# Start of an mLSTM + two-MoE kernel: clearing spread over three engines, first P ahead of the scans, unread matmuls in front

## The chip, the cores and the metric

One core of a Trainium2 chip runs the whole program. The metric is the device time of one execution in microseconds; the median of three runs of the kernel before is 531.15 us. The core has five engines that work side by side, each through its own instructions in order: TensorE (PE; its weight loads are shown as PEld), VectorE (DVE), ScalarE (ACT), GpSimd (POOL) and SyncE (SP), which here only issues transfers. They wait for each other through semaphores. On-chip memory is SBUF, and PSUM for the results of matmuls.

## The reference

Three parts, each feeding the next. The change touches only the beginning of the first, an mLSTM over 2 x 8 heads, 768 positions and a head size of 40:

```
m_new  = max(f_t + m, i_t)
C      = exp(f_t + m - m_new) * C + exp(i_t - m_new) * outer(v_t, k_t)
n      = exp(f_t + m - m_new) * n + exp(i_t - m_new) * k_t
y_t    = sigmoid(o_t) * (C q_t) / max(|n . q_t|, 1)
```

The result (1536 tokens of 320 features) goes through a mixture of 8 experts, two for each token, and then through a dense layer pair with `g = h * cos(h)`.

## The kernel before, in words

The mLSTM runs in chunks of 128 positions: six chunks for each of two batch entries, twelve steps in all, `att_step(0)` to `att_step(11)`. Inside a chunk the recurrence becomes matmuls: scores of q and k for the eight heads (`mm_s`, L247), a weight of gates for each pair of positions (`mk_w`: exponentials on ScalarE in L209, then a mask by a select on GpSimd in L210), their product P (`mk_p`, L256, on VectorE), and P times v plus the part from the state (`mm_out`, L306 and L310). `mm_state`, `mk_decay` and `mk_state` carry the state on; `mk_y` makes the output of a chunk and stores it; `rt_a` and `rt_b` do the first matmuls of the router on it.

The gates come first. `gates_a` (L82) is a row of VectorE instructions on 16 partitions: a scan for m (L90), two additions (L92, L93), a maximum (L94), and one scan per chunk for the running sum G (L96). For chunks 0 and 1, ScalarE then copies the sums (L99) into a tile that `gates_t` transposes on TensorE (L121); from chunk 2 on the sums go to DRAM instead, by a store to `gd` (L102), and come back spread over all partitions by a load of `gb` for each chunk (`load_gb`, L175). `gates_b` (L108 to L110) prepares two more rows, `gates_c` copies the transposes out (L125, L127, L128). For chunks 0 and 1, `mm_g` spreads the sums by transposes on TensorE (L196).

The order of the work is written out by hand: whatever is called first stands first in the queue of its engine. Every load and store of this stage is issued by SyncE in that order, and an issue that must wait holds up all behind it. Before step 0 the order is:

```
801  Y.dma_start(ident, cst[:, 0:128])
802  load_qk(0)   ...   load_qk(2)
808  gates_a(0, 1)  gates_b(0, 1)  gates_t(0, 1)  gates_c(0, 1)
812  mm_g(0)  mk_w(0)  mm_s(0, (0, 1))
815  gates_a(1, 2)  gates_b(1, 2)  gates_t(1, 2)
818  mm_s(0, (2, 3))
819  gates_a(2, 4)
820  gates_c(1, 2)  mk_e(0)
822  late_consts()  load_gb(2)
824  mk_p(0)
825  mm_g(1)  mk_w(1)  mm_s(1)  mk_e(1)
829  tanh_o(0)  gates_b(2, 4)
```

(Calls of several lines are drawn together here.) Step 0 then begins with the loads of chunk 3 (`loads(0)`: qk and gb of chunk 3, kv of chunk 2, the output gates of chunks 2 and 3), and each step loads ahead in the same way. The second `gates_a(4, NC)` runs at the end of step 1. Step n holds, in TensorE's order, `mm_state(n)`, the scores of chunk n + 2 interleaved with `mm_out(n)`, and the router's matmuls of chunk n - 1.

Three kinds of tiles are cleared at the start, because the loads and products fill them only in part: three qk tiles of 2048 columns (L134 to L137), two kb tiles of 512 (L141) and two st tiles of 328 (L145). GpSimd clears all of them but half of the second qk tile, which VectorE clears (L136). Each qk load waits for the clearing of its tile. `ones`, a two-byte tile for the router, is cleared at the end of step 0 (L886).

Of the kernel before, what the change touches and what calls it, by code (L numbers as in the profile page):

```python
# [9 lines left out]
FT = mybir.dt.float32  # L10
FR = mybir.dt.float32r
BF = mybir.dt.bfloat16
I32 = mybir.dt.int32
U32 = mybir.dt.uint32
AF = mybir.ActivationFunctionType
# [4 lines left out]
NH = H // 2  # L20
C = 128
# [19 lines left out]
def tile_mlstm_moe_moe2(ctx, tc, qk, kv, og, gi, gf, wcat, noise, wm1, wm2, cst, out):  # L41
    nc = tc.nc
    V, A, G, T, Y = nc.vector, nc.scalar, nc.gpsimd, nc.tensor, nc.sync

    cp = ctx.enter_context(tc.tile_pool(name="cp", bufs=1))
# [11 lines left out]
    def psS():  # L57
        return ps.tile([128, 512], FT, name="pS", tag="S", bufs=3)

    def psM():  # L60
        return ps.tile([128, 512], FT, name="pM", tag="M", bufs=1)
# [7 lines left out]
    ident = cp.tile([128, 128], FT, name="ident")  # L69
    cc_ = cp.tile([128, 341], FT, name="cc")  # L70
    A.preload_act_table_set("exp_and_others")

    g_r = cp.tile([16, C], FT, name="g_r")
    V.memset(g_r, 1.0)
# [9 lines left out]
    def gates_a(c0, c1):  # L84
        a, z = c0 * C, c1 * C
        s = slice(a, z)
        a1 = max(a, 1)
        if a == 0:
            V.memset(g_g[:, 0:1], 0.0)
        V.tensor_tensor_scan(out=g_m[:, s], data0=g_f[:, s], data1=g_i[:, s],  # L90
                             initial=(-1e30 if a == 0 else g_m[:, a - 1:a]), op0=OP.add, op1=OP.max)
        V.tensor_tensor(out=g_g[:, a1:z], in0=g_f[:, a1:z], in1=g_m[:, a1 - 1:z - 1], op=OP.add)  # L92
        V.tensor_tensor(out=g_g[:, a1:z], in0=g_g[:, a1:z], in1=g_m[:, a1:z], op=OP.subtract)  # L93
        V.tensor_scalar(g_g[:, a1:z], g_g[:, a1:z], -110.0, None, op0=OP.max)  # L94
        for c in range(c0, c1):
            V.tensor_tensor_scan(out=g_G[:, c * C:(c + 1) * C], data0=g_r, data1=g_g[:, c * C:(c + 1) * C],  # L96
                                 initial=0.0, op0=OP.mult, op1=OP.add)
        if c0 < 2:
            A.activation(gG[:, s], g_G[:, s], AF.Copy)  # L99
        if c0 >= 2:  # L100
            d0 = 0 if c0 == 2 else c0
            Y.dma_start(GD[d0:c1].rearrange("c p t -> p c t"),  # L102
                        g_G[:, d0 * C:c1 * C].rearrange("p (c t) -> p c t", t=C))
# [19 lines left out]
    def gates_c(c0, c1):  # L123
        pv = PT[c0]
        V.tensor_copy(tok[:, c0:c1, :], pv[:, :, 0:16])  # L125
        if c0 < 2:
            V.tensor_copy(tokG[:, c0:c1, :], pv[:, :, 64:80])  # L127
        A.activation(kdec[:, c0:c1, :], pv[:, :, 32:48], AF.Exp)  # L128


    NB = 3
    QKS, KBS, STS = [], [], []
    for i in range(NB):
        t = ap_.tile([128, 4, NH, C], FT, name=f"qk{i}")  # L134
        if i == 1:
            V.memset(t[:, 0:2], 0.0)  # L136
        G.memset(t[:, 2 * (i == 1):], 0.0)  # L137
        QKS.append(t)
    for i in range(2):
        t = ap_.tile([128, H, 64], FT, name=f"kb{i}")  # L140
        G.memset(t, 0.0)  # L141
        KBS.append(t)
    for i in range(2):
        t = ap_.tile([128, NH, 82], FT, name=f"st{i}")
        G.memset(t, 0.0)  # L145
        STS.append(t)
    XD = dr.tile([B * S, KW], FT, name="xd")
    KO = H * D
# [12 lines left out]
    def load_qk(n):  # L161
        if n >= 2 * NC:
            return
        b, c = divmod(n, NC)
        d = L[n]
        t = d["qk"] = QKS[n % NB]
        Y.dma_start(t[0:D, 0:3], qk[b, c, 0])
        Y.dma_start(t[64:64 + D, 1:4], qk[b, c, 1])
# [9 lines left out]
    def load_kv(n):  # L178
        if n >= 2 * NC:
            return  # L180
        b, c = divmod(n, NC)
        d = L[n]
        t = ap_.tile([128, KO + H * (D + 1)], FT, name="kv", bufs=NB)
        Y.dma_start(t, kv[b, c])
        d["k"] = t[:, 0:KO].rearrange("p (h d) -> p h d", d=D)
        d["v"] = t[:, KO:].rearrange("p (h d) -> p h d", d=D + 1)
# [26 lines left out]
    def mk_e(n):  # L213
        if n >= 2 * NC:
            return
        b, c = divmod(n, NC)
        d = L[n]
        if c:
            e = d["ge"] = ap_.tile([128, NH, C], FT, name="get", bufs=2)
            for s in range(2):  # L220
                r = slice(64 * s, 64 * s + 64)
                if n >= 2:
                    A.activation(e[r], d["gb"][r, s:H:2, :], AF.Exp)
                else:
                    for u in range(2):
                        A.activation(e[r, 2 * u:2 * u + 2, :], d["pg"][u][r, s:4:2, :], AF.Exp)
        if c < NC - 1:
            kb = d["kb"] = KBS[n % 2]
            G.tensor_tensor(out=kb[:, :, 0:D], in0=d["k"],
                            in1=kdec[:, c, b * H:b * H + H][:, :, None].to_broadcast([128, H, D]), op=OP.mult)  # L230
# [8 lines left out]
    def mm_s(n, ws=range(NH)):  # L239
        if n >= 2 * NC:  # L240
            return
        d = L[n]
        for i in ws:
            u, w = divmod(i, 2)
            if w == 0:
                d["ps", u] = psA()
            T.matmul(d["ps", u][:, 256 * w:256 * w + 256], d["qk"][:, 1, i, :],  # L247
                     d["qk"][:, 0:4:3, i, :], start=True, stop=True)

    def mk_p(n):  # L250
        if n >= 2 * NC:
            return
        d = L[n]
        d["p"] = ap_.tile([128, H, C], FT, name="ppt", bufs=2)
        for u in range(2):
            V.tensor_tensor(out=d["p"][:, 4 * u:4 * u + 4, :],  # L256
                            in0=d["ps", u].rearrange("p (h t) -> p h t", t=C),
                            in1=d["w"][:, 4 * u:4 * u + 4, :], op=OP.mult)
# [99 lines left out]


    tri = cp.tile([128, 128], BF, name="tri")  # L360
    ones = cp.tile([128, 128], BF, name="ones")
    io128 = cc_[:, 128:256]
    io32 = cc_[:, 256:288]
    tid = cc_[:, 288:300]
# [4 lines left out]
    def late_consts():  # L369
        Y.dma_start(cc_, cst[:, 128:469])  # L370
        Y.dma_start(wc, wcat)
        Y.dma_start(nz, noise)
# [426 lines left out]


    Y.dma_start(ident, cst[:, 0:128])
    load_qk(0)
    load_kv(0)
    load_qk(1)
# [11 lines left out]
    gates_b(1, 2)  # L816
    gates_t(1, 2)
    mm_s(0, (2, 3))
    gates_a(2, 4)
    gates_c(1, 2)  # L820
    mk_e(0)
    late_consts()
    load_gb(2)
    mk_p(0)
    mm_g(1)
    mk_w(1)
    mm_s(1)
# [4 lines left out]
    def loads(n):  # L832
        load_qk(n + 3)
        if n > 2 or n == 0:
            load_gb(n + 3)
        load_kv(n + 2)
        if n < 5:
            load_o(n + 1)
        if n == 2:
            load_gb(4)  # L840
            load_gb(5)

    def att_step(n):
        if n == 0:
            loads(0)
        if n:
            mk_e(n + 1)
        for f, a in pre.pop(n, []):
            f(*a)
        mm_state(n)  # L850
        if n:
            mm_s(n + 2, (0,))
        mm_out(n, (lambda w: mm_s(n + 2, (w + 1,))) if n else None)
        if n == 0:
            gates_t(2, 4)
        if n:
            rt_a(n - 1)
        mm_s(n + 2, (3,) if n else range(NH))
        for f, a in mid.pop(n, []):
            f(*a)  # L860
        if n:
            rt_b(n - 1)
        if n == 2:
            gates_t(4, NC)
        mk_state(n)
        mk_p(n + 1)
        mk_q(n + 1)
        mk_decay(n + 1)
        if n == 0:
            gates_c(2, 4)  # L870
        if n == 2:
            gates_c(4, NC)
        if n == 1:
            gates_a(4, NC)
        loads(n + 1)
        if n == 2 * NC - 1:
            mk_y(n)
        for f, a in fill.pop(n, []):
            f(*a)
        if n < 2 * NC - 1:  # L880
            mk_y(n)
        mk_w(n + 2)
        if n == 0:
            V.tensor_copy(tri, cc_[:, 0:128])
            V.tensor_copy(rb[:, 0], row0)
            V.memset(ones, 1.0)  # L886
            V.memset(os_[:, NC], 0.0)
        if n == 1:
            gates_b(4, NC)
        if n == 8:  # L890

            for p, r0, st, m in ((64, ROW0[2] + CAP2, 512, 6), (16, CAP1, 256, 2), (16, ROW1[0] + CAP1, 256, 2)):
                Y.dma_start(bass.AP(tensor=YD.tensor, offset=YD.offset + r0 * DM, ap=[[DM, p], [st * DM, m], [1, DM]]),
                            cc_[:p, None, 0:DM].to_broadcast([p, m, DM]))
# [84 lines left out]
    for f in range(12):  # L979
        k = 18 + (15 * f) // 4  # L980
# [19 lines left out]
    for k in range(K0, KM + N2 + 2):  # L1000
# [6 lines left out]
        while at.get(k):  # L1007
            f, a = at[k].pop(0)
# [8 lines left out]
    with tc.If(over > 0):  # L1017
# [9 lines left out]
        for b in range(B):  # L1027
            with tc.For_i(0, NC, 1) as it:
# [4 lines left out]
                p = psM()  # L1033
# [6 lines left out]
                for e in range(E):  # L1040
                    acc = psA()
                    for f in range(8):
                        w = mp.tile([128, FW], FT, name="wr", tag="wh", bufs=4)
                        Y.dma_start(w, wm1[e, :, f, :])
                        p = psS()
                        for k in range(3):
                            n = 64 if k == 2 else 128
                            T.matmul(p[:, :C], w[:n, 128 * k:128 * k + 128], xT[:n, 128 * k:128 * k + 128],
                                     start=(k == 0), stop=(k == 2))
# [10 lines left out]
                for f in range(16):  # L1060
                    wh, wl = W2[f // 4][:, 0, f % 4, :], W2[f // 4][:, 1, f % 4, :]
                    p = psS()
# [6 lines left out]
                t = mp.tile([128, DM], FT, name="yt", tag="yt", bufs=3)  # L1069
# [76 lines left out]
```

## Time and profile before

| | |
|---|---|
| three runs | 530.97, 531.15, 532.72 us |
| median | 531.15 us |
| profiled execution | 531.55 us |
| its span, first to last instruction | 529.9 us |
| granted TensorE clock, mean | 0.988 of full |
| TensorE busy | 494.5 us, 93% of the span |
| VectorE, ScalarE, GpSimd busy | 372.7, 325.7 and 282.2 us |

The profile is one execution, and it stands 0.4 us above the median; 1.65 us of it lie around the span. Times in its rows are counted from the first instruction. Matmuls are pipelined, so a busy TensorE need not be at its best rate. The attention stage fills about the first hundred microseconds; the experts and the dense pair, where TensorE is almost always busy, follow.

### The profile page before, as it was taken

The page shows a single profiled execution, that of the slowest core. Times are in us where ns is not written, and L with a number is a line of the kernel's source. Part 1 is how long each engine was busy: PE and PEld are TensorE (multiplying, and loading weights), DVE is VectorE, ACT ScalarE, POOL GpSimd, SP SyncE. Part 2 cuts the span into 40 slices and gives each one's busy share as a digit, 9 for nine tenths or more (in the row PEclk, how much of TensorE's full clock was granted, in tenths as well). Part 3 has the DMA queues.
Part 4 walks back from the last instruction along what each step waited for, and adds up shares of the span by engine and source line. Part 5 has one row for each costly group of instructions (what it writes and reads, how often), then busy time and mean ns, then how long its engine had stood idle before and what let it go on. Part 6 is the DMA issues. An engine that isn't in the chain of part 4 may idle for free.

```text
span 529.9 us, 9037 instructions
## 1 busy us (share of the span) xinstructions
PE 494.5 (93%) x3198; PEld 471.0 (89%) x3198; DVE 372.7 (70%) x789; ACT 325.7 (61%) x695; POOL 282.2 (53%) x248
## 2 busy tenths in 40 slices
PE   4898988898999999999999988999999999999994
PEld 2787876798999999999999987899899999999994
DVE  8874379567467776878776679678956755787772
ACT  3667565464646454545455556478777777777772
POOL 6445457668755968585868597264356347300000
PEclk9999898999999999999999998999999999999999
DMA  6889894467183928391938194030021003001001
GB/s 192 249 265 277 286 285 147 140 220 272 61 301 130 343 84 280 127 357 58 340 139 271 74 344 152 15 115 26 0 63 51 1 1 100 12 2 37 2 1 44
DMA packets 25909, 77.69 MB, mean 147 GB/s; under 512 B 3872, under 2 KB 11552, under 8 KB 25856
## 3 DMA queue, kind: packets, MB, share of 16 engines
q1 hardware_dynamic: 22752, 67.50, 36.9%
q0 software_dynamic: 3104, 9.54, 5.9%
q8 instruction: 27, 0.44, 0.3%
q14 instruction: 26, 0.21, 0.1%
HBM read 67.41 MB, written 9.62 MB: 145 GB/s over the span
## 4 chain that ended last, share of the span: by engine, by line
PE 73%; DVE 12%; ACT 5%; DMA 4%; issue 3%; POOL 1%; SPq 0%; POOLq 0%; DVEq 0%; ACTq 0%
PE pS L582 33%; PE pA L591 10%; PE pA L588 9%; PE pA L587 9%; PE pS L310 2%; PE pM L544 2%; PE pA L247 2%; DMA qk<-qk 2%; PE pA L600 1%; PE pA L599 1%; ACT wt L209 1%; PE pM L351 1%; DVE xt L667 1%; PE pS L306 1%; DMA wraw<-wm 1%
## 5 line engine op out<-in xcount | busy, mean ns | idle before, releaser
L575 POOL TENSOR_TENSOR wl<-wraw,wh 128x704 fp32r<-128x704 f32 x71 | 125.9, 1781 | 61.7 <-ACT wh L573 58.9
L637 DVE SCALAR_TENSOR_TENSOR hb<-pS,hb 128x384 fp32r<-128x384 f32 (+2 forms) x128 | 45.9, 390 | 46.3 <-ACT hb L634 43.8
L573 ACT ACTIVATE wh<-wraw 128x704 fp32r<-128x704 f32 x80 | 62.9, 786 | 15.9 <-PE pA L599 7.5
L582 PE MATMUL pS<-xh,wh 128*128 128x448 f32 (+1 forms) x240 | 69.8, 345 | 0.7 <-ACT xh L546 0.5
L582 PE MATMUL pS<-xh,wl 128*128 128x448 f32 (+1 forms) x240 | 66.6, 332 | 0.9 <-POOL wl L575 0.9
L582 PE MATMUL pS<-xh,w 128*128 128x384 f32 x288 | 66.5, 339 | 0.6 <-DVE m_t L747 0.6
L587 PE MATMUL pA<-wh,hb 128*128 128x320 f32 x208 | 62.7, 311 | 0.0
L588 PE MATMUL pA<-wl,hb 128*128 128x320 f32 x208 | 62.6, 310 | 0.0
L732 ACT ACTIVATE m_t<-pS,magic 128x384 f32<-128x384 f32 x64 | 37.1, 580 | 30.3 <-PE pS L582 25.5
L634 ACT ACTIVATE hb<-pS 128x448 fp32r<-128x448 f32 (+1 forms) x80 | 37.7, 471 | 28.8 <-PE pS L582 22.0
L582 PEld LDWEIGHTS pS<-xh,w 128*128 128x128 f32 x288 | 50.0, 188 | 1.2 <-DVE m_t L747 1.1
L591 PE MATMUL pA<-wh,hb 128*128 128x320 f32 x208 | 44.6, 314 | 3.0 <-DVE hb L637 3.0
L747 DVE SCALAR_TENSOR_TENSOR m_t<-m_t,pS 128x384 f32<-128x384 f32 x64 | 35.4, 553 | 15.4 <-ACT m_t L746 13.5
L582 PEld LDWEIGHTS pS<-xh,wl 128*128 128x128 f32 x240 | 43.2, 191 | 3.3 <-POOL wl L575 1.1
L733 DVE TENSOR_SCALAR m_t<-m_t 128x384 f32<-128x384 f32 x64 | 23.4, 365 | 28.8 <-ACT m_t L732 27.8
L582 PEld LDWEIGHTS pS<-xh,wh 128*128 128x128 f32 x240 | 40.9, 190 | 1.9 <-ACT xh L546 0.6
L753 POOL TENSOR_TENSOR wl<-m_t,wh 128x384 fp32r<-128x384 f32 x25 | 25.5, 1019 | 30.9 <-ACT wh L751 21.4
L582 PE MATMUL pS<-xl,wh 128*128 128x448 f32 (+1 forms) x160 | 39.7, 329 | 0.0
L588 PEld LDWEIGHTS pA<-wl,hb 128*128 128x128 f32 x208 | 39.0, 188 | 0.5
L587 PEld LDWEIGHTS pA<-wh,hb 128*128 128x128 f32 x208 | 38.9, 187 | 0.7
L591 PEld LDWEIGHTS pA<-wh,hb 128*128 128x128 f32 x208 | 33.3, 187 | 4.9 <-DVE hb L637 4.9
L734 DVE SCALAR_TENSOR_TENSOR m_t<-pS,m_t 128x384 f32<-128x384 f32 x64 | 35.7, 558 | 2.2
(197 smaller groups left out, 1253.7 us busy)
## 6 DMA issues: line engine op xcount, KB each, us to landing
wraw<-wm SPq DMA_DIRECT2D x36, 704.0 KB
raw<-wm SPq DMA_DIRECT2D x16, 704.0 KB
qk<-qk SPq DMA_DIRECT2D x24, 240.0 KB
gb<-gd SPq DMA_DIRECT2D x10, 512.0 KB
kv<-kv SPq DMA_DIRECT2D x12, 324.0 KB
yd<-yt SPq DMA_DIRECT2D x22, 160.0 KB
wraw<-wm SPq DMA_DIRECT2D x8, 352.0 KB
xd<-xt SPq DMA_DIRECT2D x12, 192.0 KB
```

The lines of the kernel that those rows point to most:

```text
L573: A.activation(wh, raw[:, f, :], AF.Copy)
L575: eng.tensor_tensor(out=wl, in0=raw[:, f, :], in1=wh.bitcast(FT), op=OP.subtract)
L582: T.matmul(p[:, :n], w[:, 128 * k:128 * k + 128], x[:, m, :], start=(i == 0), stop=(i == 7))
L587: T.matmul(a[:n, :DM], hh[:, s], wh[:, KW:], start=first, stop=False)
L588: T.matmul(a[:n, :DM], hh[:, s], wl[:, KW:], start=False, stop=False)
L591: T.matmul(a[:n, :DM], hl[:, s], wh[:, KW:], start=False, stop=last)
L634: A.activation(hh[:, :n], p[:, :n], AF.Relu)
L637: V.scalar_tensor_tensor(out=hb[:, o:o + z - a], in0=p[:, a:z], scalar=0.0, in1=hh[:, a:z].bitcast(FT), op0=OP.max, op1=OP.subtract)
L732: A.activation(t, m["p"], AF.Identity, bias=magic, scale=0.5 / PI)
L734: V.scalar_tensor_tensor(out=t, in0=m["p"], scalar=0.5 / PI, in1=t, op0=OP.mult, op1=OP.subtract)
L747: V.scalar_tensor_tensor(out=s, in0=s, scalar=1.0, in1=m["p"], op0=OP.subtract, op1=OP.mult)
L753: eng.tensor_tensor(out=m["hl"], in0=m["t"], in1=m["hh"].bitcast(FT), op=OP.subtract)
```

## The change

At the start, `ones` is cleared first on VectorE. The clearing is dealt out anew: GpSimd clears the first qk tile and half of the second; ScalarE clears the other half of the second and all of the third, by three copies of a zero column spread over 1024 columns; VectorE clears the zero column, kb and st. Before the first loads are issued, fourteen matmuls of `ones` with itself (384 columns each) go to TensorE, into a PSUM tile that nobody reads. And `mk_p(0)` moves from behind `late_consts` and `load_gb(2)` to just behind `mk_e(0)`, while `gates_a(2, 4)` moves from ahead of `gates_c(1, 2)` to behind `mk_p(0)`.

```diff
+    ones = cp.tile([128, 128], BF, name="ones")
+    V.memset(ones, 1.0)
...
+    zero = cp.tile([128, 1], FT, name="zero")
+    V.memset(zero, 0.0)
     for i in range(NB):
         t = ap_.tile([128, 4, NH, C], FT, name=f"qk{i}")
-        if i == 1:
-            V.memset(t[:, 0:2], 0.0)
-        G.memset(t[:, 2 * (i == 1):], 0.0)
+        if i == 0:
+            G.memset(t, 0.0)
+        else:
+            if i == 1:
+                G.memset(t[:, 0:2], 0.0)
+            for k in range(2 * (i == 1), 4, 2):
+                v = t[:, k:k + 2].rearrange("p a w t -> p (a w t)")
+                A.activation(v, zero.to_broadcast([128, 2 * NH * C]), AF.Copy)
         QKS.append(t)
     for i in range(2):
         t = ap_.tile([128, H, 64], FT, name=f"kb{i}")
-        G.memset(t, 0.0)
+        V.memset(t, 0.0)
...
         t = ap_.tile([128, NH, 82], FT, name=f"st{i}")
-        G.memset(t, 0.0)
+        V.memset(t, 0.0)
...
     Y.dma_start(ident, cst[:, 0:128])
+
+    junk = psM()
+    for i in range(14):
+        T.matmul(junk[:, 0:384], ones, ones[:, None, :].to_broadcast([128, 3, 128]), start=True, stop=True)
     load_qk(0)
...
     mm_s(0, (2, 3))
-    gates_a(2, 4)
     gates_c(1, 2)
     mk_e(0)
+    mk_p(0)
+    gates_a(2, 4)
     late_consts()
     load_gb(2)
-    mk_p(0)
     mm_g(1)
...
-            V.memset(ones, 1.0)
```

## Rows read from the trace of the kernel before

**Rows 1.** The chain that ended last, by engine (the page's part 4).

```profile
PE 73%; DVE 12%; ACT 5%; DMA 4%; issue 3%; POOL 1%; SPq 0%; POOLq 0%; DVEq 0%; ACTq 0%
```

**Rows 2.** Busy time by stretch; the last three columns: granted clock, DMA share, GB/s.

```profile
17.00:26.00 9.00, 7.86 (x60) 7.26 (x59) 7.05 (x20) 5.79 (x18) 5.18 (x9) 1.00 0.99 310
29.00:31.00 2.00, 2.00 (x20) 1.95 (x19) 0.88 (x4) 1.31 (x6) 0.00 (x0) 1.00 0.40 105
31.00:43.00 12.00, 11.37 (x86) 10.12 (x86) 8.05 (x18) 8.82 (x24) 6.87 (x12) 1.00 0.98 293
...
53.00:57.00 4.00, 4.00 (x19) 3.68 (x19) 1.14 (x2) 0.38 (x1) 1.18 (x2) 0.57 0.95 276
```

**Rows 3.** Timeline, TensorE: start, duration, instruction, idle before it and its releaser.

```profile
23.62 0.67 PE L247 MATMUL pA<-qk 128*128 128x256 f32 x2 [0.86 <-DVE st L293]
...
51.81 0.67 PE L247 MATMUL pA<-qk 128*128 128x256 f32 x2 [1.81 <-DMA qk<-qk]
...
66.27 0.30 PEld L247 LDWEIGHTS pA<-qk 128*128 128x128 f32 x2 [0.27 <-issue]
```

**Rows 4.** Timeline, SyncE's issues of transfers.

```profile
14.14 0.33 SPq L102 DMA_DIRECT2D gd<-g_all  x1
...
16.16 0.33 SPq L175 DMA_DIRECT2D gb<-gd  x1
...
28.85 0.34 SPq L102 DMA_DIRECT2D gd<-g_all  x1
```

**Rows 5.** Timeline, the clearing on VectorE and GpSimd.

```profile
0.82 4.45 POOL L137 MEMSET qk<- 128x2048 f32 x3 [0.29 <-POOLq L1139]
...
2.16 0.91 DVE L136 MEMSET qk<- 128x1024 f32 x1 [0.16 <-issue]
```

**Rows 6.** Timeline, the gates and the first P on VectorE.

```profile
3.34 0.41 DVE L90 TENSOR_TENSOR_SCAN g_all<-g_all 16x128 f32<-16x128 f32 x1 [0.26 <-DMA g_all<-gi]
...
4.41 1.38 DVE L94 TENSOR_SCALAR g_all<-g_all 16x127 f32<-16x127 f32 x1
...
8.86 0.21 DVE L94 TENSOR_SCALAR g_all<-g_all 16x128 f32<-16x128 f32 x1
...
10.36 1.05 DVE L90 TENSOR_TENSOR_SCAN g_all<-g_all 16x256 f32<-16x256 f32 x1
...
13.38 0.73 DVE L96 TENSOR_TENSOR_SCAN g_all<-g_r,g_all 16x128 f32<-16x128 f32 x2
...
14.19 1.27 DVE L256 TENSOR_TENSOR ppt<-pA,wt 128x512 f32<-128x512 f32 x2
...
15.38 0.40 DVE L108 TENSOR_TENSOR g_all<-g_all 16x256 f32<-16x256 f32 x1
...
25.38 0.73 DVE L90 TENSOR_TENSOR_SCAN g_all<-g_all 16x256 f32<-16x256 f32 x1
```

**Rows 7.** Timeline, TensorE: transposes, the two-byte matmuls of L497, long ones of L582.

```profile
7.87 1.97 PE L196 MATMUL pS<-ident,tokG 128*128 128x128 f32 x8 [0.35 <-DVE tokG L127]
...
11.58 0.40 PE L121 MATMUL pM<-ident,g_all 80*128 80x80 f32 x1
...
14.31 1.09 PE L196 MATMUL pS<-ident,tokG 128*128 128x128 f32 x8 [1.26 <-DVE tokG L127]
...
91.65 0.51 PE L497 MATMUL pM<-r_bm,r_am 128*128 128x64 bf16 x12 [0.27 <-ACT Lt L355]
...
142.91 0.36 PE L582 MATMUL pS<-xh,wh 128*128 128x448 f32 x1
143.11 0.36 PE L582 MATMUL pS<-xh,wl 128*128 128x448 f32 x1
```

**Rows 8.** Timeline, ScalarE: exponentials of chunks 0 and 2, and a 640-column activation.

```profile
9.02 2.18 ACT L209 ACTIVATE wt<-pS,tok 128x128 f32<-128x128 f32 x8 [0.92 <-PE pS L196]
...
18.36 0.74 ACT L157 ACTIVATE ogt<-ogt 128x640 f32<-128x640 f32 x1
...
20.69 2.44 ACT L209 ACTIVATE wt<-gb,tok 128x128 f32<-128x128 f32 x8
```

More of the change, by code (lines that the diff above doesn't have):

```diff
@@ L360, in tile_mlstm_moe_moe2 @@
     tri = cp.tile([128, 128], BF, name="tri")
-    ones = cp.tile([128, 128], BF, name="ones")
     io128 = cc_[:, 128:256]
```

## The prediction

> **What bounds the kernel now.** I read the chain of waits first, then the share of the DMA engines by stretch, then the waits in the timeline that the first two point to. The chain says that the whole run belongs to TensorE, 73% of it [rows 1]. That share is an average: the change touches only the first 25 us, so what counts there is which wait ends last, and what a shift there does to the rest.
>
> In the attention stage the transfers run without a pause. The sixteen DMA engines are 0.99 busy from 17 to 26 us and 0.98 from 31 to 43 [rows 2]. The one hole is 29 to 31 us, at 0.40. TensorE meets this stream three times: it waits 0.86 us at 23.62 before it may start the scores of chunk 3, 1.81 us at 51.81 and 0.27 us at 66.27 [rows 3]. The row at 51.81 names the qk load. The one at 23.62 names a VectorE instruction of L293, but `mk_state(1)` stands behind `mm_s(3, (0,))` in the code and can't hold it; what that matmul needs is its qk load, so I read this as the load too. The row at 66.27 names nothing; it is again the first score matmul of a step.
>
> What starts the stream is one instruction. SyncE issues in order, and the store of the gate sums to `gd` (L102) waits for the scans of chunks 2 and 3 on VectorE. It goes out at 14.14; the first `gb` load, which reads `gd` back, at 16.16 [rows 4]; behind it stand the loads of chunk 3 and all later ones. The next `gd` store, at 28.85, closes the hole at 29 to 31. So the time at which VectorE ends `gates_a(2, 4)` sets when the stream starts, and I follow the change to that point.
>
> **VectorE up to the first scan.** Removed is the clearing of half of qk1, 1024 columns in 0.91 us, 0.89 ns per column [rows 5]. Added are kb (2 x 512) and st (2 x 328), 1680 columns, 1.50 us at that price; `ones`, 128 columns, between 0.11 by the same price and 0.17 where it stood before, and `zero`, some 0.06. That is about 0.75 us more. The first scan (3.34 us) had waited 0.26 for the load of gi [rows 6], which is now covered, so it starts 0.5 later, at 3.85.
>
> **The stalled maximum.** The 127-column maximum of L94 took 1.38 us at 4.41, the same instruction for chunk 1 only 0.21 at 8.86 [rows 6]. It stood beside GpSimd's clearing, which went on without a break from 0.82 past 5 us [rows 5]. Now GpSimd clears 3072 columns instead of 6800, of which 5120 took the 4.45 us of their row, and is done at about 3.5, before L94 runs. I take the whole 1.17 as saved; the other end is nothing, if the stall had another cause. Net, the gates of chunk 0 are ready 0.65 earlier.
>
> **The unread matmuls.** The eight transposes of chunk 0, among the first work of TensorE, take 1.97 us, those of chunk 1 only 1.09 [rows 7]. The profile gives the granted clock as full here, but the ratio is that of its two levels, 1.2 and 2.4 GHz. Fourteen matmuls of 384 columns ahead of them should bring the full level, as the matmuls between the two rows did. Their own price isn't shown. Long matmuls of L582, 448 columns, start 0.20 apart at the full level; that is 0.17 for 384 columns and 0.34 at half the clock. The two-byte matmuls of L497, 64 columns in 0.51/12 us, give 0.26, and at half the clock 0.51 [rows 7]. I take 0.34, as the row nearest in length: 4.8 us from 1.1, over at 5.9, ahead of the gates at 6.5. At 0.51 they end at 8.2 and put off everything behind by 1.6; that end goes into the range. Were they full from the start, they would end at 3.5, which changes nothing unless the pause behind them brings the low level back. The gain at full clock is half of the 0.88 before the first exponentials of chunk 0, which start at 7.9 instead of 9.02: 1.1 earlier.
>
> **ScalarE's clearing** costs the path nothing: three copies of 1024 columns at 0.74 us per 640 columns [rows 8] are at most 3.5 us, from 2.4 to 5.9. Their cover is that ScalarE has next to nothing to do before the gates of chunk 0 are ready at 6.5. If they run over, the copy of L99 and, in SyncE's queue, the qk load of chunk 2 are late by a few tenths, and chunk 2's scores are not wanted before 18. For the clearing of `ones`, gone from the end of step 0, nothing is booked either: VectorE was not awaited there once the load of chunk 3 is.
>
> **P in front of the scans.** ScalarE needs 2.18 us for the exponentials of chunk 0 [rows 8] and only then copies the gate sums of chunk 1 (L99), which the transposes wait for. Those stood at 11.58 [rows 7] and come at 10.5. VectorE ends `gates_b(1, 2)` at about 9.7, used to go on with the scans of chunks 2 and 3 at 10.36, and now stands idle until the two copies of `gates_c(1, 2)` at 10.9. Then comes `mk_p(0)`, 1.27 us, from 11.0 to 12.3. Only then the scans start, 2.0 later than before; `mk_p` itself issues no transfer, but the scans take the `gd` store with them, and behind it on SyncE the three loads of constants, `gb` of chunk 2 and everything of step 0.
>
> The scan block took 3.75 us (10.36 to 14.11). Undisturbed, its five kinds cost 0.73 (L90 at 25.38), 0.40 twice (by L108's shape), 0.25 (L94, between rows) and 0.73 (L96), with the gaps 2.65 [rows 6]; so the three GpSimd instructions beside it cost 1.1, as the scan of L90 shows (1.05, against 0.73 undisturbed). In the new place two of GpSimd's selects for chunk 1 fall on it, 0.37 each: 3.4. The block ends at 15.7; the bounds are 14.95 undisturbed and 16.05 at the old price.
>
> The Trainium skill (SBUF — State Buffer, "Who interferes with whom") says that a VectorE instruction with two SBUF inputs and a GpSimd instruction that reads SBUF take turns, and that the one issued later waits for the whole other one. By that rule, an estimate, the block would be 2.65 if VectorE is first each time. The slow and the quick L90 agree with the rule; who comes first in the new place no row can tell.
>
> So `gd` goes out at about 15.7 instead of 14.14, **1.5 later**. What is earlier buys nothing there: the transposes of chunk 1, free of the scans, move from 14.31 to 11.6 and their exponentials with them, but step 1 waits for chunk 3's load.
>
> **What is late next.** The first `gb` load moves to 17.7, the exponentials of chunk 2 that read it from 20.69 [rows 8] to at most 22.2, TensorE's start at 23.62 to 25.1. Between the end of these exponentials (23.13) and the next scans (25.38) lie a select, products and some slack, which I put at 0.5 (an estimate). So the second `gd` store moves by 1.0, and with it the stream from 31 us on, which has no hole left that would take it up: 51.81 and 66.27 move by 1.0. TensorE, idle from about 20.5 to 25.1, will run at the low level for a while: after the 1.81 us pause its granted clock was 0.57 from 53 to 57 [rows 2], which lost 1.7 us. Its step 1 then ends some 3 us late; but it has 1.8 to give at 51.81, and where it no longer waits there, the fall at 53 to 57 goes too. So at 66.27 it waits for the loads again, and the shift is the stream's.
>
> **The sum**: the profiled execution took 531.55 us (span 529.9, 1.65 around it); with 1.0 more 532.55. It stands 0.4 above the median of 531.15, so the forecast is 532.1.
>
> **Rivals.**
> *The loads keep up (faster).* If the stream makes good the late start, TensorE goes by its own work. For it: transposes and exponentials of chunk 1 come 2.7 earlier, and the stream takes no more than 1 us of TensorE's time in the first 40. Against it: 0.99 busy. Place: TensorE at 23.62; it decides where chunk 3's load is there before 22.8. The gain lies between the 0.86 waited there and 2.7; 1.8 gives 529.4.
> *A further fall of the clock (slower).* If TensorE reaches 66.27 with nearly 2 us to wait, it falls to the low level once more, as it did behind the pause of 1.81 us. That adds 1.7 to the shift: 533.8. Against it: step 7 has slack in VectorE's router work.
> *Nothing happens.* The hole at 29 to 31 is 1.2 us of transfer time. If it takes up all of the shift, or the L94 gain is larger than I think, both ends meet: 531.2.
>
> **How the numbers follow.** Forecast 0.4, loads keep up 0.2, further fall 0.2, nothing 0.2. The range goes from 529.3, the fast rival, to 534.6, the second fall with long unread matmuls; a bit under 2 in 10 is left out. Within 0.3% is 1.6 us either way, about what can be told from no change. Faster by more: most of the fast rival and a little of low bounds, 0.2. Slower by more: nearly all of the further fall and a quarter of the forecast's own spread, 0.3. Same: 0.5.
>
> **What would show it.** In the changed kernel: L94 near 0.2 us at about 5; the first transposes in 1.1 us; `mk_p(0)` ahead of L90 at 12.3; L102 at 15.0 to 16.1; the score matmul of chunk 3 at about 25; no low clock at 53 to 57. The forecast is wrong if L102 comes before 14.5, or if it is late and the matmul at 23.6 is not.

## The result and the profile after

The change made the kernel slower: a median of 537.04 us against 531.53 us of the kernel before, six executions each, ratio 1.0101 with a 95% interval of 1.0066 to 1.0136. That lies above the forecast's range. The same program, measured once more beside the experiments, gave 1.0079 (1.0034 to 1.0123).

| | before | after |
|---|---|---|
| profiled execution | 531.55 us | 535.83 us |
| its span | 529.9 us | 534.1 us |
| granted TensorE clock, mean | 0.988 | 0.976 |
| TensorE busy | 494.5 us | 498.8 us |

The program adds only fourteen short matmuls to TensorE, which are busy for 3.7 us, and yet its span grew by 4.2 us. The chain of waits of the kernel after, by engine, gives DMA 7% where it had 4% [rows 1]:

```profile
PE 72%; DVE 11%; DMA 7%; ACT 3%; issue 3%; POOL 1%; SPq 1%; DVEq 0%; POOLq 0%; ACTq 0%
```

The timeline of the kernel after, from the start to the first `gb` load (its lines answer to [rows 4, 6, 7, 8]; line numbers have moved by 2 to 9):

```profile
1.14 3.73 PE L813 MATMUL pM<-ones 128*128 128x384 bf16 x14 [1.14 <-DVE ones L73]
...
3.86 0.41 DVE L92 TENSOR_TENSOR_SCAN g_all<-g_all 16x128 f32<-16x128 f32 x1
...
4.93 0.21 DVE L96 TENSOR_SCALAR g_all<-g_all 16x127 f32<-16x127 f32 x1
...
6.67 0.26 PE L123 MATMUL pM<-ident,g_all 80*128 80x80 f32 x1 [1.80 <-DVE g_all L112]
...
7.28 1.97 PE L205 MATMUL pS<-ident,tokG 128*128 128x128 f32 x8 [0.35 <-DVE tokG L129]
...
8.43 2.17 ACT L218 ACTIVATE wt<-pS,tok 128x128 f32<-128x128 f32 x8 [0.93 <-PE pS L205]
...
11.48 1.50 DVE L265 TENSOR_TENSOR ppt<-pA,wt 128x512 f32<-128x512 f32 x2
...
12.89 0.73 DVE L92 TENSOR_TENSOR_SCAN g_all<-g_all 16x256 f32<-16x256 f32 x1
...
13.87 0.70 POOL L219 TENSOR_SCALAR_AFFINE_SELECT wt<-wt 128x512 f32<-128x512 f32 x1 [1.87 <-ACT wt L218]
...
14.89 0.76 POOL L219 TENSOR_SCALAR_AFFINE_SELECT wt<-wt 128x512 f32<-128x512 f32 x1 [0.32 <-ACT wt L218]
15.19 1.53 DVE L98 TENSOR_TENSOR_SCAN g_all<-g_r,g_all 16x128 f32<-16x128 f32 x2
15.62 0.82 POOL L238 TENSOR_TENSOR kb<-kv,kdec 128x320 f32<-128x320 f32 x1
...
16.75 0.34 SPq L104 DMA_DIRECT2D gd<-g_all  x1
...
18.59 0.38 SPq L184 DMA_DIRECT2D gb<-gd  x1
```

Up to 6.67 it is better than before: the stalled maximum is gone (0.21 against 1.38), and the gates of chunk 0 reach TensorE about 0.5 us earlier. Then the first P (11.48) stands ahead of the scans (12.89), three GpSimd instructions fall on the scans, and the `gd` store goes out at 16.75, 2.61 later than before.

The timeline further on: TensorE's score matmuls of chunks 3 and 9 and the state matmuls of steps 2 and 8, SyncE's issues of the second `gd` and of the qk load of chunk 6, and ahead of the latter VectorE's product `qtt` of chunk 3 (`mk_q`), the last reader of the tile that it fills:

```profile
26.19 1.19 PE L256 MATMUL pA<-qk 128*128 128x256 f32 x2 [4.29 <-DMA qk<-qk]
...
30.31 0.34 SPq L104 DMA_DIRECT2D gd<-g_all  x1
...
34.41 0.88 PE L275 MATMUL pS<-kv,kb 128*104 128x82 f32 x8
...
39.92 0.75 DVE L246 TENSOR_TENSOR qtt<-qk,get 128x512 f32<-128x512 f32 x1
40.74 0.31 SPq L176 DMA_DIRECT2D qk<-qk  x1
...
69.89 1.19 PE L256 MATMUL pA<-qk 128*128 128x256 f32 x2 [2.49 <-DVE pM L403]
...
79.07 0.94 PE L275 MATMUL pS<-kv,kb 128*104 128x82 f32 x8
```

In the kernel before, the first score matmul and the second `gd` stand in [rows 3, 4]; the others are:

```profile
29.47 0.88 PE L266 MATMUL pS<-kv,kb 128*104 128x82 f32 x8
...
34.97 0.75 DVE L237 TENSOR_TENSOR qtt<-qk,get 128x512 f32<-128x512 f32 x1
35.80 0.31 SPq L167 DMA_DIRECT2D qk<-qk  x1
...
66.30 0.67 PE L247 MATMUL pA<-qk 128*128 128x256 f32 x2
...
73.91 0.94 PE L266 MATMUL pS<-kv,kb 128*104 128x82 f32 x8
```

And busy time by stretch of the kernel after (TensorE's busy time and instructions stand after the length; the last three columns are granted clock, DMA share and GB/s):

```profile
7.30:9.00 1.70, 1.70 (x8) 1.70 (x9) 1.56 (x6) 0.75 (x4) 0.00 (x0) 0.50 1.11 356
...
22.00:26.00 4.00, 0.00 (x0) 0.00 (x0) 2.35 (x9) 3.20 (x10) 1.50 (x3) 0.78 0.95 283
26.00:32.00 6.00, 5.81 (x25) 5.36 (x26) 4.15 (x8) 0.39 (x1) 0.80 (x1) 0.58 0.84 304
50.00:60.00 10.00, 9.59 (x71) 8.53 (x71) 4.87 (x11) 7.20 (x20) 4.86 (x8) 1.00 0.89 268
68.00:76.00 8.00, 6.12 (x25) 5.61 (x26) 5.93 (x33) 3.44 (x10) 3.36 (x5) 0.57 0.93 291
```

TensorE now waits 4.29 us for chunk 3's load where it had waited 0.86 [rows 3], and behind that wait two score matmuls take 1.19 us and not 0.67: it runs at the lower of its two levels (0.58 granted from 26 to 32). The wait of 1.81 at 51.81 and the low clock behind it [rows 2, 3] are gone, 50 to 60 us is at full clock. But at 69.89 comes a second long wait, 2.49 us, and a second fall. That row names a VectorE instruction of the router (L403), which a score matmul does not read; what it reads is the qk tile, so I take it for the qk load of chunk 9, which the same row names in a run below (66.38).

So the way of the lateness along TensorE is: +2.57 at the scores of chunk 3 (26.19 against 23.62); +4.94 at the state matmuls of step 2 (34.41 against 29.47), as the way between them takes 8.22 us and not 5.85; only +1.25 at step 7 (66.52 against 65.27), since the old wait and fall are gone; +3.59 at the scores of chunk 9 (69.89 against 66.30); +5.16 at step 8 (79.07 against 73.91), as the way there takes 9.18 us and not 7.61. What comes behind gives back about 1 us of it, which I didn't follow up; 4.2 is left at the end.

### The profile page after: what moved, and what is told of

It is laid out like the page before. It is cut to its first block, busy times and chain, and to the rows that moved or that the text cites. A ratio compares the mean times of both kernels' runs of the same rounds, so it can differ in the third digit from the quotient of the medians.

```text
span 534.1 us, 9067 instructions
## 1 busy us (share of the span) xinstructions
PE 498.8 (93%) x3212; PEld 473.8 (89%) x3212; DVE 372.1 (70%) x793; ACT 328.4 (61%) x698; POOL 279.1 (52%) x243
## 4 chain that ended last, share of the span: by engine, by line
PE 72%; DVE 11%; DMA 7%; ACT 3%; issue 3%; POOL 1%; SPq 1%; DVEq 0%; POOLq 0%; ACTq 0%
PE pS L590 32%; PE pA L599 10%; PE pA L595 9%; PE pA L596 9%; DMA gb<-gd 3%; PE pM L552 2%; PE pS L319 2%; PE pA L256 2%; DMA wraw<-wm 1%; PE pA L608 1%; PE pA L607 1%; DMA xgt<-xd,idx 1%; DMA qk<-qk 1%; PE pM L360 1%; ACT wt L218 1%
## 5 line engine op out<-in xcount | busy, mean ns | idle before, releaser
L256 PE MATMUL pA<-qk 128*128 128x256 f32 x96 | 32.9, 443 | 8.7 <-DMA qk<-qk 4.3
```

## The experiments

Each run was timed against the kernel before on the same chip. That kernel's executions there went from 527.8 to 539.7 us, a wider spread than in the first measurement, so tenths of a per cent can't be told apart by one run. The interval of a single run doesn't cover all of it either: the clearing alone, measured on two chips, gave two that don't meet (below).

**Which part costs?** Four kernels, each with a part of the change. First the change with P left where it was:

```diff
-    mk_p(0)
-    gates_a(2, 4)
     late_consts()
     load_gb(2)
+    mk_p(0)
...
     mm_s(0, (2, 3))
+    gates_a(2, 4)
     gates_c(1, 2)
```

> The changed kernel with the old order of mk_p(0) and gates_a(2, 4): the clearing and the unread matmuls alone. Queue theory (P ahead of the scans puts off the gd store, and with it all loads behind it; TensorE's longer waits then drop its clock): the gd store goes out at 13.4 to 13.8 us instead of 16.75, the first matmul of chunk 3's scores at about 23, and the time is that of the kernel before or a little under, 530.5 to 531.5 us. Rival (the clearing on VectorE and ScalarE or the unread matmuls cost the time): the time stays at 535 us or more though the gd store is early.

Measured: 532.84 us, ratio 0.9977 (0.9946 to 1.0008), `gd` at 13.64. The loss is gone with the move. The scores of chunk 3 start at 24.77, not at about 23, because the first `gb` load goes out only at 17.47 (the section on the prediction comes back to this). The reverse, only the move of P and the scans on the kernel before:

```diff
-    gates_a(2, 4)
     gates_c(1, 2)
     mk_e(0)
+    mk_p(0)
+    gates_a(2, 4)
     late_consts()
     load_gb(2)
-    mk_p(0)
```

> The kernel before with mk_p(0) ahead of gates_a(2, 4), nothing else. Queue theory: scans of chunks 2 and 3 start at about 13.6 us, the gd store goes out at 17.2 to 17.6 (0.5 to 0.9 later than in the changed kernel, since the stall of L94 is still there), and the time is 536 to 539 us, as slow as the whole change or slower. Rival: below 533.5 us.

Measured: 537.41 us, 1.0046 (1.0009 to 1.0083): slower, with `gd` 3.6 later than before and the same long wait ahead of the scores of chunk 3 (its row names VectorE's product P, which a score matmul does not read either). Its timeline, SyncE's `gd` and TensorE's score matmuls:

```profile
17.74 0.33 SPq L102 DMA_DIRECT2D gd<-g_all  x1
...
27.91 1.19 PE L247 MATMUL pA<-qk 128*128 128x256 f32 x2 [4.99 <-DVE ppt L256]
...
72.87 0.67 PE L247 MATMUL pA<-qk 128*128 128x256 f32 x2 [2.62 <-DMA qk<-qk]
```

The two other parts alone, the clearing and the unread matmuls (each as in the change's diff):

```diff
-        G.memset(t[:, 2 * (i == 1):], 0.0)
+                A.activation(v, zero.to_broadcast([128, 2 * NH * C]), AF.Copy)
...
-        G.memset(t, 0.0)
+        V.memset(t, 0.0)
```

> The kernel before with the new division of the clearing, nothing else. Queue theory: L94 of chunk 0 takes 0.2 instead of 1.4 us, the gd store goes out about 0.6 earlier, near 13.5, and the time is 530.5 to 531.5 us. Rival (clearing on VectorE or ScalarE costs): 533 us or more, with qk loads or the first scan late.

```diff
+    junk = psM()
+    for i in range(14):
+        T.matmul(junk[:, 0:384], ones, ones[:, None, :].to_broadcast([128, 3, 128]), start=True, stop=True)
```

> The kernel before with the clearing of ones and the fourteen unread matmuls at the start, nothing else. Queue theory: they end at 4.9 us, TensorE then stands still for over 2 us and the first transposes run at the low clock as before (about 1.97 us for eight); gd store within 0.3 us of 14.14; time within 1 us of the kernel before. Rival (the unread matmuls move the falls of the clock): a fall less or more than before, and 1.5 us or more in either direction.

Measured: the clearing alone 530.45 us, 0.99 (0.9863 to 0.9937), `gd` at 13.34, 0.80 earlier than before; the unread matmuls alone 531.17 us, 0.9964 (0.9929 to 1.0), `gd` at 14.16 as before. Neither costs anything. The move of P is the part that does; whether it makes the whole loss by itself (1.0046 against 1.0101 and 1.0079) the spread doesn't tell.

**By which way does a late `gd` cost?** In the kernel after, the qk load of chunk 3 was issued by SyncE ahead of the scans, so that it no longer stands behind the `gd` store; then the same in the kernel before:

```diff
+    load_qk(3)
     gates_a(2, 4)
...
     def loads(n):
-        load_qk(n + 3)
+        if n:
+            load_qk(n + 3)
```

> The kernel after, with the qk load of chunk 3 issued by SyncE ahead of the scans of chunks 2 and 3 and not behind the gd store. Theory (the late gd store holds the qk load of chunk 3, TensorE waits 4.3 us for it and then runs at the low clock): gd stays late, at 16.5 to 17.5, but the two qk issues come at 11 to 14; the first score matmul of chunk 3 comes at 22 to 23.5 instead of 26.19, with no wait for a qk load above 1 us there, the granted clock between 24 and 31 us rises well above the 0.5 to 0.57 of the kernel after, and 2 to 4 us of the time come back: 533 to 535 against 537. Rival (what is lost lies in the scans and P themselves, or in the unread matmuls and the clearing): the matmul comes early, but TensorE then waits as long for another link (gb, the second P), and the time stays at 536 to 538.

> The kernel before with the same early qk load. It shows what the early load is worth where gd is not late, so that it can be taken off the run beside it. Theory: the wait of 0.86 us at 23.62 goes and the scores of chunk 3 start at 22.5 to 23; gd stays at 14.1 to 14.5, the gb loads land within 0.5 us of before; the time is 0 to 1.5 us less than before (ratio 0.997 to 1.000). Rival (the row at 23.62 was not the load but VectorE): the start stays at 23.6, ratio 1.000.

Measured: in the kernel after 533.76 us, 1.0011 (0.9981 to 1.0041). The loss is gone although `gd` is nearly as late as it was. The timeline, the early load, `gd` and the scores of chunk 3, which now follow the state matmuls without a wait:

```profile
11.74 0.28 SPq L176 DMA_DIRECT2D qk<-qk  x1
...
16.28 0.33 SPq L104 DMA_DIRECT2D gd<-g_all  x1
...
22.97 0.64 PE L256 MATMUL pA<-qk 128*128 128x256 f32 x2
```

One wait and one fall of the clock are left further on (3.11 us at 44.79, 0.57 granted from 46 to 50), and yet the state matmuls of step 8 start at 74.27, only 0.36 later than before. So what the late `gd` does, it does through the load behind it. In the kernel before the same edit gained nothing: 534.72 us, 1.0023 (0.9996 to 1.0050), against my expectation. Its timeline:

```profile
14.14 0.34 SPq L102 DMA_DIRECT2D gd<-g_all  x1
...
19.06 0.80 SPq L175 DMA_DIRECT2D gb<-gd  x2
...
67.43 1.19 PE L247 MATMUL pA<-qk 128*128 128x256 f32 x2 [2.20 <-DVE xt L327]
```

The wait at 23.62 did go, but the first `gb` load, which needs the `gd` store to have landed, goes out at 19.06 and not at 16.16 [rows 4], as I read it because the early load now stands ahead of the store in the transfers; the second `gd` is 1.6 late (30.45), and a wait with a fall of the clock comes at 67.43 in place of that at 51.81. The early load moved the lateness and did not remove it. The clearing alone with the early load:

> The kernel before with the new clearing alone (no unread matmuls, P where it was) and the early qk load of chunk 3. Theory: gd at 13.3 to 13.7, scores of chunk 3 at 21.8 to 22.6 without a wait for a load, and the time below that of the clearing alone: ratio to before 0.985 to 0.993, faster than both kernels. Rival (transfers later in the stream decide, not chunk 3's load): no more than the clearing alone gave, 0.99 to 0.997.

Measured: 532.71 us, 0.9993 (0.9962 to 1.0023), `gb` at 18.93: the rival was right, the early load adds nothing to the clearing.

**How much of it is the clock?** The kernel after, with unread matmuls of 128 columns where TensorE waits, in steps 1 and 7. The loads are as late as they were:

```diff
+    FILL = {1: 72, 7: 40}
...
         mm_state(n)
+        if n in FILL:
+            L[n]["po"] = psS()
+            for i in range(FILL[n]):
+                T.matmul(L[n]["po"][:, 384:512], ones, ones, start=True, stop=True, skip_group_check=True)
```

> The kernel after, with further unread matmuls between mm_state and the score matmuls of steps 1 and 7 (72 and 40 of 128 columns), where TensorE waits 4.3 and 2.5 us for qk loads. The loads are as late as they were; what changes is what TensorE does meanwhile. Theory (two falls of the clock behind the waits are a part of the loss): the scores of chunk 3 still come at 26 to 26.5, but the granted clock behind them is 0.9 or more instead of 0.5 to 0.57, steps 2 to 4 are 2.4 to 3.2 us later than before instead of 4.95, the fall at 68 to 76 is gone, and the time is 533 to 535. Rival (the late loads alone set the time, the clock has slack): the clock is full but the shift from 74 us on stays above 4.5 us and the time at 536 to 537.5.

Measured: 533.73 us, 1.0013 (0.9987 to 1.0039). The loss is gone although the scores of chunk 3 come later still, at 27.54 and not at 26 to 26.5, `gd` goes out at 16.86, and step 2 is 3.93 later than before, more than the 2.4 to 3.2 expected. Its timeline, scores of chunk 3 and the state of step 2:

```profile
27.54 0.67 PE L256 MATMUL pA<-qk 128*128 128x256 f32 x2 [1.50 <-DMA qk<-qk]
...
33.40 0.88 PE L275 MATMUL pS<-kv,kb 128*104 128x82 f32 x8
```

Between these two rows lie 5.86 us, as in the kernel before (5.85) and not 8.22: without the fall of the clock, step 1 costs what it did. That gives the price of a fall: 2.37 us in step 1 of the kernel after, and 3.82 in its second measurement (26.74 to 36.41). For the second, the way from the scores of chunk 9 to the state of step 8 is 6.49 here (68.54 to 75.03) and 9.18 in the kernel after, 2.69 more.

Each fill alone tells how the two hang together:

```diff
-    FILL = {1: 72, 7: 40}
+    FILL = {1: 72}
```

> The kernel after with the unread matmuls of step 1 alone (72), behind which the clock fell first. If the first fall is the costly one, step 2 is 3.9 us later than before and not 4.95 to 6.9, and most of the 3.5 us that both fills gave come back: 533 to 534.5. If the second fall is the costly one, steps 2 to 4 gain 1 us or more, but from 66 us on the shift is again above 4 us and the time 535.5 to 537.5.

```diff
-    FILL = {1: 72, 7: 40}
+    FILL = {7: 40}
```

> The kernel after with the unread matmuls of step 7 alone (40). If the second fall is the costly one, steps 2 to 4 stay 5 to 7 us late, steps 6 and 7 at 1 to 3.3, and from 74 us on the shift stays below 3 us, with the granted clock there at 0.95 or more: 533 to 535. If the first fall is the costly one, 535.5 to 537.5.

Measured: step 1 alone 533.54 us, 1.0000 (0.9965 to 1.0036); step 7 alone 533.55 us, 1.0011 (0.9981 to 1.0041). Either is enough. The timelines, first of the fill in step 1:

```profile
26.36 0.67 PE L256 MATMUL pA<-qk 128*128 128x256 f32 x2 [0.88 <-DVE ppt L265]
...
66.38 0.67 PE L256 MATMUL pA<-qk 128*128 128x256 f32 x2 [1.19 <-DMA qk<-qk]
```

then of the fill in step 7:

```profile
25.60 0.67 PE L256 MATMUL pA<-qk 128*128 128x256 f32 x2 [4.15 <-DMA qk<-qk]
...
33.11 0.88 PE L275 MATMUL pS<-kv,kb 128*104 128x82 f32 x8
...
68.17 0.65 PE L256 MATMUL pA<-qk 128*128 128x256 f32 x2
```

With step 1 filled, TensorE reaches step 2 earlier, the loads behind it are issued earlier (chunk 6 at 38.54 and not 40.74, chunk 9 at 57.20 and not 59.32), and at 66.38 it waits 1.19 and not 2.49, without a fall behind it. With step 7 filled the first fall stays (7.51 us to step 2 and not 5.85), though step 2 comes 3.64 later than before and not 5 to 7 as expected, but the second is gone. So the loss of the kernel after shows at the second wait, and the first fall is what makes that wait long. One reservation: in both profiles the transposes of chunk 0 ran fast and `gd` went out at 16.29, half a microsecond earlier than in the kernel after (the last section tells why), so single rows differ by that much beside the edit; the medians of twelve executions carry the verdict.

The kernel after was measured once more, and beside it with more unread matmuls at the start:

> The kernel after, unchanged, measured together with the three beside it, so that they can be compared with it. By both theories gd goes out at 16.5 to 17, the scores of chunk 3 at 25.5 to 26.5 and the ratio to before is 1.006 to 1.014, as it was. If it were within 0.2% of before here, the loss first measured would hang on the executions and not on the program.

Measured: 537.2 us, 1.0079 (1.0034 to 1.0123), `gd` at 16.71, scores of chunk 3 at 26.74: as before, so that the fills and the early load are compared with a loss that stands. They ran on two other chips, so what is compared is each one's ratio to the kernel before: 1.0000 to 1.0013 for the four cures, 1.0079 and 1.0101 for the kernel after.

```diff
-    for i in range(14):
+    for i in range(25):
```

> The kernel after with 25 unread matmuls and not 14, so that they end at about 6.7 and not at 4.87, where the gates are ready. Theory (a pause of 1.8 us behind the unread matmuls brought the low clock back, and at the low clock the scores of chunk 0 are late, P waits for them and the scans behind P): the eight transposes take 1.0 to 1.3 us and not 1.97, the first exponentials start at 7.3 to 7.9 and not at 8.43, P is 1.25 to 1.35 us, gd goes out 0.8 to 1.2 earlier, at 15.5 to 16.0, the scores of chunk 3 at 24.5 to 25.3, and the time is 1 to 3 us below the kernel after. Rival (the slow transposes are not the clock's, or P waits for something else): transposes at 1.97, gd at 16.5 to 17 and the time as after. A case between: gd earlier by 1, the time not, if the wait of 4.3 us only becomes 3.3 and the clock falls all the same.

Measured: 538.56 us, 1.0102 (1.0048 to 1.0155). Half of the expectation fell, and the time with it. The timeline:

```profile
1.14 7.18 PE L813 MATMUL pM<-ones 128*128 128x384 bf16 x25 [1.14 <-DVE ones L73]
...
9.03 1.09 PE L205 MATMUL pS<-ident,tokG 128*128 128x128 f32 x8 [0.35 <-DVE tokG L129]
...
18.04 0.34 SPq L104 DMA_DIRECT2D gd<-g_all  x1
```

The transposes take 1.09 and not 1.97, as the theory has it. But the unread matmuls stood 0.32 apart until 7.18, where in the kernel after they sped up at about 3.7, so they ended past 8 and held up the gates behind them; `gd` is 1.3 later than in the kernel after. A filler that waits for nobody can itself become what is waited for.

**A version that beats both?** The clearing alone once more, and with fills in steps 7 and 9, where its profile showed the clock falling; beside it the kernel before with fills in steps 5 and 9 (edits as above):

> The new clearing alone once more, beside the two parts of the filled kernel. If its gain is real the ratio to before is again below 0.997, near the 0.99 first measured and the 0.995 of the same kernel with filled waits; if that was the executions' spread, 0.998 to 1.003. gd at 13.3 to 13.5 either way.

> The kernel before with the new clearing alone, and unread matmuls of 128 columns in step 7 (44) and step 9 (30), where its profile shows TensorE waiting 2.8 and 1.9 us and the granted clock at 0.57 from 66 to 70 and 0.68 to 0.89 from 80 to 88. Theory (each fall of the clock costs 1.5 us or so beside the wait): clock at 0.95 or more there, 1.5 to 3 us below the clearing alone: 527.5 to 529.5 where before is 531.5, ratio 0.985 to 0.993. Rival (TensorE would have waited for loads and for VectorE anyway, so a quicker TensorE waits longer at the next place): no less than the clearing alone, 0.99 to 0.998.

> The kernel before with such unread matmuls in step 5 (30) and step 9 (30), where it waits 1.8 and 1.9 us: what two falls of the clock cost in the kernel before. Theory: granted clock at 53 to 57 and 84 to 88 at 0.95 or more and not 0.57 and 0.59, ratio 0.993 to 0.998. Rival (behind the wait the loads are the bound, and the low clock has slack): clock full, ratio 0.999 to 1.002.

Measured: the clearing alone 532.37 us, 0.9982 (0.9944 to 1.0021), an interval that does not meet that of its first measurement (0.9863 to 0.9937), so that its gain isn't settled; with fills 530.19 us, 0.9952 (0.9917 to 0.9986), below the kernel before with its interval and, at the median, 7 us below the kernel after measured beside it, though its distance to the clearing alone can't be told. The kernel before with fills: 531.71 us, 0.9993 (0.9959 to 1.0028). Its stretches show why nothing came of it:

```profile
53.00:57.00 4.00, 3.80 (x29) 3.29 (x28) 1.24 (x2) 0.98 (x2) 1.28 (x2) 1.00 0.97 253
66.00:70.00 4.00, 2.99 (x10) 2.75 (x11) 3.67 (x28) 2.72 (x8) 1.41 (x3) 0.63 1.03 282
```

The fall at 53 to 57 is gone (1.00 against 0.57 in [rows 2]), but TensorE, being earlier, waits 2.34 us at 67.01, and the clock falls there. There the fall that was taken away only moved to the next wait; filling clearly paid only in the kernel after, where TensorE was late at the end of the stage.

## Why the prediction was wrong, step by step

Right: what bounds the start. A late `gd` puts off the start of the stream, its lateness reaches TensorE at the scores of chunk 3 (`gd` 2.61 later, the scores 2.57), the wait of 1.81 and its fall of the clock vanish (predicted by the step on what is late next), and what comes earlier in the gates of chunk 1 buys nothing. The first scan came at 3.86 (3.85 predicted), the maximum of L94 took 0.21, and ScalarE's clearing (2.17 to 5.1 us) cost nothing, as the clearing alone shows. One line was misread: the row at 66.27 [rows 3] names no releaser, and the scores start at 66.30, 0.15 behind the state matmuls of step 7 (65.27, 0.88 long). The kernel before shows no wait for a load there, though the prediction counts it as the third meeting with the stream.

**The unread matmuls**: half wrong. I had them at one distance of 0.34 and ending at 5.9, with full clock behind them. They ran 0.32 apart and then at double rate, ended at 4.87, TensorE stood idle for 1.80 us, and behind that it was at the low level: the granted clock is 0.50 from 7.3 to 9, the transposes took 1.97. The text named this pause and booked nothing for it; that the pause alone decides is not shown (the last section has two runs with the same pause and different transposes). The first exponentials came 0.59 earlier (8.43), not 1.1.

**P in front of the scans**: right in kind, short in size. `gd` came at 16.75, not 15.7, above the upper bound of 16.05, which only let the scans vary. The 1.05 are three terms: 0.5 of the exponentials above, through the copy of L101 and the transposes of chunk 1 (P at 11.48 and not 11.0); some 0.1 in P; and 0.43 in the scans, 3.83 us and not 3.4, because not two but three GpSimd instructions fell on them, the `kb` product (15.62) among them; the price of 0.37 for each was about right. By the rule that a VectorE instruction with two SBUF inputs contends with a GpSimd instruction that reads SBUF (the Trainium skill, SBUF — State Buffer, "Who interferes with whom"), the prediction put 2.65 if VectorE is first each time. The rows agree with the rule in that the two L98 scans beside the select and the product took 1.53 against 0.73 undisturbed, and at 3.83 VectorE was not first each time.

**What is late next**: this is the step that failed. I let the second `gd` move by 1.0 and took that as the shift of all later loads. It moved by 1.46 (30.31), and the loads behind it by far more: the qk load of chunk 6 went out at 40.74, and in the kernel before at 35.80. That is 4.94, exactly TensorE's own lateness at step 2. The stream is not a clock of its own: three qk tiles go round, and the load of chunk 6 waits for the last reader of chunk 3's tile, VectorE's product in step 2, which ends at 40.67 and not at 35.72. I had seen that step 1 would end some 3 us late at the low clock (it became 4.94: 2.57 of the late load and 2.37 of the clock, where the text had 1.5 and 1.7) and let it be absorbed at 51.81. It was, on TensorE; but the loads issued in the meantime had taken the lateness with them, and chunk 9's scores started 3.59 later, not 1.0.

**The further fall**, given 0.2, is what happened. Its condition, nearly 2 us of waiting at 66.27, came true with 2.49, its price of 1.7 was 1.57 in the profile against the kernel before (9.18 against 7.61). With the shift of 3.59 in place of 1.0, that makes the 5.16 at step 8. Either cure, of the load, of the first fall or of the second, takes the time back to within 0.2% of the kernel before; the rival's sentence against it, that step 7 has slack in VectorE's router work, held for about 1 us of the fall's 2.69: in the kernel before TensorE waits 0.93 us for the router at 71.40, and in the kernel after it doesn't.

What stays open: the clearing and the earlier gates should be worth about 0.8 us by the profile; three measurements (0.9900, 0.9952 with fills, 0.9982) point that way without settling its size, and with the early load it is 0.9993. One reason can be seen. In the two profiles of the clearing alone `gd` goes out at 13.34 and at 13.35, but the first `gb` load so:

```profile
15.19 0.38 SPq L182 DMA_DIRECT2D gb<-gd  x1
...
17.06 0.33 SPq L182 DMA_DIRECT2D gb<-gd  x1
```

In the first of them the DMA engines are 0.29 busy from 13 to 15 us, in the second 0.68. I read this so: where the first loads are still on their way, an earlier `gd` does not start the stream earlier. The scores of chunk 3 start at 22.79 in the one and at 24.44 in the other.

## What to carry to other kernels

Before moving work ahead of an instruction that feeds a transfer, follow the transfer to the engine that waits for it, and then follow that engine's lateness back into the loads that its own steps issue: with a small ring of buffers the two feed each other, and the shift at the next meeting is not the first one's. Charge a long wait of TensorE with the low clock behind it (here 1.6 to 3.8 us beside the wait), and test it with unread matmuls in the wait, which cost little and tell clock from load; but size them to end before what comes next. Not every long wait has a fall behind it. In the second profile of the clearing alone

```profile
24.44 0.67 PE L254 MATMUL pA<-qk 128*128 128x256 f32 x2 [2.48 <-DVE ppt L263]
```

is followed by 1.00 granted from 26 to 32 us, and a wait of 1.83 us at 65.83 in the change with P left where it was by 1.00 from 66 to 70, where 1.81 us in the kernel before was followed by 0.57 [rows 2, 3]. So the clock behind each wait has to be read. Issuing one load earlier in a full stream can delay another (19.06 and 18.93 for the first `gb` load, against 16.16).

## What the runs showed of the hardware beyond what was expected

The time at which TensorE reached full speed at the start differed between executions of the same instructions. In the kernel after, the fourteen unread matmuls were busy for 3.73 us; in the run with the early load, for 4.53 us, and the pause behind them was 1.00 us and not 1.80. The transposes were fast there (1.09) and slow in the kernel after. With step 7 alone filled, the unread matmuls took 4.66 us, the pause was 0.87, and the transposes of chunk 0 took 1.09:

```profile
1.14 4.66 PE L813 MATMUL pM<-ones 128*128 128x384 bf16 x14 [1.14 <-DVE ones L73]
...
7.27 1.09 PE L205 MATMUL pS<-ident,tokG 128*128 128x128 f32 x8 [0.35 <-DVE tokG L129]
```

With both waits filled, the matmuls and the pause were the same, and the transposes took 1.97 again:

```profile
1.14 4.66 PE L813 MATMUL pM<-ones 128*128 128x384 bf16 x14 [1.14 <-DVE ones L73]
...
7.38 1.97 PE L205 MATMUL pS<-ident,tokG 128*128 128x128 f32 x8 [0.35 <-DVE tokG L129]
```

In that last run the profile grants 1.00 from 7.30 to 9.00, while the same eight transposes take 1.09 us elsewhere: at the very start the durations tell the level and the granted clock does not, as in the kernel before [rows 7].
